# The second expert layer as one Strassen-type product over four experts, on one Trainium2 core

## The chip, the core and the metric

The kernel runs on one core of a Trainium2 chip. The core has engines that work side by side: TensorE (PE, with its weight loads listed apart as PEld), VectorE (DVE), ScalarE (ACT), GpSimd (POOL) and SyncE (SP, which here only issues DMAs). They wait for each other through semaphores. Matrix products are written to PSUM; DVE and ACT read them from there and write to SBUF. The metric is the time of one execution on the device in microseconds (us); smaller is better.

## What is computed

Attention over eight sorted blocks, whose output goes through a layer of four experts that are all used and mixed with normalised weights p. There are four batches of 768 tokens, 8 heads of 64, a model width of 512 and a hidden width of 1024.

```python
def _attn_ref(q, k, v, sort_net):
    ...
    for _ in range(5):
        P = P - np.max(P, axis=-1, keepdims=True)
        P = np.exp(P)
        P = P / (np.sum(P, axis=-1, keepdims=True) + 1e-09)
        P = P / (np.sum(P, axis=-2, keepdims=True) + 1e-09)
    k_sorted = np.einsum('bhij,bhjcd->bhicd', P, k_b).reshape(B, H, S, D)
    v_sorted = np.einsum('bhij,bhjcd->bhicd', P, v_b).reshape(B, H, S, D)
    ...
    scores = scale * np.matmul(q_b, k_sb.transpose(0, 1, 2, 4, 3))
    ...
    return np.matmul(attn, v_sb).reshape(B, H, S, D).astype(np.float32)

def _moe_ref(x, domain_probs, w1, w2):
    p = domain_probs / (domain_probs.sum(-1, keepdims=True) + 1e-09)
    ...
    for e in range(E):
        h = np.maximum(x @ w1[e], 0.0)
        out += p[:, e:e + 1] * (h @ w2[e])
    return out.astype(np.float32)
```

## The kernel before

All four experts' weights are brought to SBUF in f16 (`load_w1` and `load_w2`, lines 94 to 98) by DMAs that POOL issues. So are q, k and v of a batch (`load_natural`, line 79), in tiles with two buffers of a whole batch each, so that the next batch is loaded while one is worked on.

The attention of a batch is cut into small stages: `st_v`, `st_q`, `st_k` bring v, q and k into the layouts needed, `st_s` makes the scores and their exponentials, `st_a` the weighted sums, which `normalize` (line 334) divides on DVE, and `st_x` transposes the result into `xT`, the input of the experts. `attention_order` (line 464) lists the 24 stages of a batch. Batch 0 has stages of its own (`h_k` to `h_x`) that work on half a batch (`hf`).

`expert` (line 488) computes one expert for 768 tokens (`hf` is None, batches 1 to 3) or for 384 (batch 0). The first layer takes w1 as the stationary operand and 384 tokens as the moving one; after eight matmuls ACT writes relu of the two PSUM banks to `hT` as f16 (lines 504 and 520). The second layer takes 128 tokens of `hT` as the stationary operand and 512 columns of w2 as the moving one, sums eight matmuls in a PSUM bank, and DVE adds p times that to `oacc` (lines 535 and 539). After the last expert the rows go to DRAM from SP's queue.

`run` (line 555) threads the attention stages of the next batch into the experts of the present one: after each piece of expert work it calls `slot`, which issues as many stages as keep pace with the share of expert work done. The kernel is scheduled by hand: each engine executes its instructions in the order in which they are written. Lines 590 to 621 are the outer order: POOL builds the sort matrices (`build_PI`, lines 232 to 251) and loads what comes next, then batch 0's units run in two calls of `run`, then batches 1 to 3 in one call each. Batch 3's has no stages left to thread in.

PSUM has two pools of two buffers, each of two banks: `psM` for the experts and `psA` for attention.

Of the kernel before, what the change touches and what calls it, by code (L numbers as in the profile page):

```python
# [17 lines left out]
def kernel(  # L18
# [41 lines left out]
    moeo = ctx.enter_context(tc.tile_pool(name="moeo", bufs=9))  # L60
# [18 lines left out]
    def load_natural(b, nm, lo, n, p0=0, pn=P):  # L79
# [4 lines left out]
        nc.gpsimd.dma_start(  # L84
            t[ds(p0, pn), ds(lo, n), :, :].rearrange("p h r d -> p h (r d)"),
            src[b, ds(lo, n)].rearrange("h (p r) d -> p h (r d)", r=R)[ds(p0, pn)],
        )

# [11 lines left out]
    load_natural(0, "k", 0, 4)  # L100
    load_natural(0, "q", 0, 4, 0, P // 2)
# [4 lines left out]
    load_natural(0, "v", 0, 4)  # L106
    load_natural(0, "k", 4, 4)
    load_natural(0, "v", 4, 4)
    load_natural(0, "q", 4, 4, 0, P // 2)
    load_natural(0, "q", 0, H, P // 2, P // 2)  # L110
# [10 lines left out]
    )  # L121
    kTs, ETs, vos, vs0s = [], [], [], []
# [8 lines left out]
    for n in range(2):  # L131
        vs0 = att.tile([BLK, HB, 2, 2, VW], F16, name=f"vs0_{n}", tag="vs")
        nc.gpsimd.memset(vs0[:, :, :, :, ds(D, 2)], 1.0)
        vs0s.append(vs0)
# [3 lines left out]
    load_w2(1)  # L138
    nc.gpsimd.tensor_copy(
# [3 lines left out]
    for n in range(2):  # L143
# [26 lines left out]
    def q_half(b, pr, hf, copy):  # L170

        ps = psa([P, R, 64], F16, f"ps_q_{b}_{pr}_{hf}")
        for r in range(R):
            for hh in range(2):
                nc.tensor.transpose(
                    ps[ds(D * hh, D), r, :],
                    natural[(b, "q")][ds(64 * hf, 64), 2 * pr + hh, r, :],
                    ident[ds(64 * hf, 64), ds(64 * hf, 64)],
                )
        if (b, pr) not in qTs:  # L180
            qTs[(b, pr)] = att.tile([P, NB, R * CP], F16, name=f"qT_{b}_{pr}", tag="qT", bufs=4)
        copy(
            qTs[(b, pr)][:, ds(HB * hf, HB), :].rearrange("p i (r c) -> p i r c", r=R),
            ps.rearrange("p r (i c) -> p i r c", c=CP),
        )
# [36 lines left out]
    PI0 = [const.tile([P, H, HB, CP], F16, name=f"PI0_{a}") for a in range(2)]  # L222
# [11 lines left out]
    def build_PI(eng, n, which):  # L234
        r4 = Rs[:, ds(4 * n, 4), :]
        if which == "k":
            PIk[n] = att.tile([P, 4, NB, CP], F16, name=f"PIk_{n}", tag="PIk", bufs=4)
            eng.tensor_tensor(  # L238
                PIk[n][:],
                maskk.rearrange("p (o i c) -> p o i c", o=1, c=CP).broadcast_to([P, 4, NB, CP]),  # L240
                r4.rearrange("p g (i o) -> p g i o", o=1).broadcast_to([P, 4, NB, CP]),
                ALU.mult,
            )
        else:
            PIv[n] = att.tile([P, 4, CP, NB], F16, name=f"PIv_{n}", tag="PIv", bufs=4)
            eng.tensor_tensor(
                PIv[n][:],
                maskv.rearrange("p (o c i) -> p o c i", o=1, i=NB).broadcast_to([P, 4, CP, NB]),
                r4.rearrange("p g (o i) -> p g o i", o=1).broadcast_to([P, 4, CP, NB]),
                ALU.mult,  # L250
            )
# [8 lines left out]

    def st_v(b, pr):
        ps = psa([P, 2, 512], F32, f"ps_v_{b}_{pr}")
        for hh in range(2):
            h = 2 * pr + hh
            nc.tensor.matmul(  # L265
                ps[:, hh, 0:R * D],
                PIv[(b * H + h) // 4][:, h % 4, :, :].rearrange("p c i -> p (c i)"),
                natural[(b, "v")][:, h, :, :].rearrange("p r d -> p (r d)"),
                start=True, stop=True,
            )  # L270
        vo = vos[pr // 2]
        nc.vector.tensor_copy(  # L272
            vo[:, :, ds(2 * (pr % 2), 2), 0:D],
            ps[:, :, 0:R * D].rearrange("p h (r d) -> p r h d", r=R),
        )
        if pr % 2:
            qd = pr // 2
            nc.sync.dma_start(
                vs_dram[b, qd].rearrange("r c i x -> (c i) r x"),
                vo.rearrange("p r h w -> p r (h w)"),  # L280
            )
            vs = att.tile([BLK, NB, 4, VW], F16, name=f"vs_{b}_{qd}", tag="vs")
            nc.sync.dma_start(
                vs.rearrange("c i h w -> c (i h w)"),
                vs_dram[b, qd].rearrange("r c i x -> (r c) (i x)"),
            )
            vss[(b, qd)] = vs

    def st_q(b, pr):
        ps = psa([P, R, P], F16, f"ps_q_{b}_{pr}")  # L290
        for r in range(R):
            for hh in range(2):
                nc.tensor.transpose(  # L293
                    ps[ds(D * hh, D), r, :], natural[(b, "q")][:, 2 * pr + hh, r, :], ident[:]
                )
        qT = att.tile([P, NB, R, CP], F16, name=f"qT_{b}_{pr}", tag="qT", bufs=4)
        nc.vector.tensor_copy(qT[:], ps.rearrange("p r (i c) -> p i r c", c=CP))  # L297
        qTs[(b, pr)] = qT.rearrange("p i r c -> p i (r c)")

    def st_k(b, pr):  # L300
        ps = psa([P, R, P], F32, f"ps_k_{b}_{pr}")
        for r in range(R):
            for hh in range(2):
# [3 lines left out]
                    natural[(b, "k")][:, h, r, :],  # L307
# [4 lines left out]
        nc.vector.tensor_copy(  # L312
# [49 lines left out]
    def st_x(b, pr):  # L362
# [8 lines left out]
        nc.vector.tensor_copy(  # L371
# [7 lines left out]
    vT0, xsl0 = {}, {}  # L379

    def mix_half(nm, qd, hf, dst, copy):

        ps = psa([P, 2, R, 64], F32, f"ps_m{nm}_{qd}_{hf}")
        for sg in range(2):
            for r in range(R):
                for hh in range(2):
# [3 lines left out]
                        natural[(0, nm)][:, h, r, :],  # L390
# [11 lines left out]
    def h_v(qd, hf):  # L402
        vT = att.tile([P, S], F16, name=f"vT_{qd}_{hf}", tag="vT")
        vT0[(qd, hf)] = vT
        mix_half("v", qd, hf, vT, nc.scalar.copy)

    def h_w(qd, hf):
        ps = psa([BLK, 2 * HB, P], F16, f"ps_w_{qd}_{hf}")
        vT = vT0[(qd, hf)]
# [54 lines left out]
    def attention_order(b):  # L464
# [11 lines left out]
        return [lambda f=f, pr=pr: f(b, pr) for f, pr in o]  # L476


    def mix_weights():
# [4 lines left out]
        nc.vector.tensor_tensor(p_sb[:], p_sb[:], den[:].broadcast_to([P, B, R, E]), ALU.mult)  # L484

    oaccs = {}

    def expert(b, e, hf, slot):

        n = S if hf is None else HS  # L490
        hT = moe.tile([P, NFC, n], F16, name=f"hT_{b}_{e}_{hf}", tag="hT")
        if hf is None:
            xT = xTs[b].rearrange("p k r i c -> p k (r i c)")
            for fc in range(NFC):
                ps = psm([P, 2, 512], F32, f"ps_h_{b}_{e}_{fc}")
                for nh in range(2):
                    for kc in range(NKC):
                        nc.tensor.matmul(  # L498
                            ps[:, nh, 0:HS],
                            w1sb[e][:, kc, ds(fc * P, P)],  # L500
                            xT[:, kc, ds(nh * HS, HS)],
                            start=(kc == 0), stop=(kc == NKC - 1),
                        )
                nc.scalar.activation(  # L504
                    hT[:, fc, :].rearrange("p (a x) -> p a x", a=2), ps[:, :, 0:HS],
                    AF.Relu, bias=0.0, scale=1.0,
                )
                slot()
        else:
# [14 lines left out]
        for t in range(n // P):  # L524
            col = t if hf is None else (R // 2) * hf + t
# [17 lines left out]
            if e == E - 1:  # L543
                oacc = oaccs[(b, col)]
                if hf is None:
                    nc.sync.dma_start(
                        out[ds(b * S, S), :].rearrange("(p r) d -> p r d", r=R)[:, t, :], oacc[:]
                    )
                else:
                    o = out[ds(b * S + hf * HS, HS), :].rearrange("(p r s) d -> p r s d", r=R // 2, s=2)  # L550
                    for s2 in range(2):
                        nc.sync.dma_start(o[:, t, s2, :], oacc[ds(64 * s2, 64), :])
            slot()

    def run(units, fill, spare=4):

        slots = sum((NFC + R) if hf is None else (NFC // 2 + R // 2) for _, _, hf in units)
# [8 lines left out]
        for b, e, hf in units:  # L566
            expert(b, e, hf, slot)
        for f in fill:
            f()

# [37 lines left out]
    run([(0, 0, 0), (0, 1, 0)], second, 2)  # L608
    run(
        [(0, 0, 1), (0, 1, 1), (0, 2, 0), (0, 2, 1), (0, 3, 0), (0, 3, 1)],  # L610
        attention_order(1),
    )
    for b in range(1, B):
        if b + 1 < B:
            for nm in ("k", "v", "q"):
                load_natural(b + 1, nm, 0, H)
        if b + 2 < B:
            for n in range(2 * b + 4, 2 * b + 6):
                build_PI(nc.gpsimd, n, "v")
                build_PI(nc.gpsimd, n, "k")  # L620
        run([(b, e, None) for e in range(E)], attention_order(b + 1) if b + 1 < B else [])


# [28 lines left out]
```

## Time and profile before

| | |
|---|---|
| median of 3 runs | 416.14 us (413.9 to 416.29) |
| the profiled execution | 414.46 us |
| its span, first to last instruction | 412.6 us |
| mean granted TensorE clock | 0.982 |
| batch 0, with the attention of batch 1 | 0 to 137.1 us |
| batches 1 and 2, with attention of the next | 137.1 to 231.4, 231.4 to 325.8 us |
| batch 3, experts alone | 325.8 to 412.6 us |

The profile is one execution, recorded by the hardware. A group row reads: line, engine, operation, output<-input by the program's names, partitions x elements and type, count | busy time in us, mean ns of one | idle time of the engine before them, and what ended most of it. The chain that ended last is read from the last instruction back: at each step stands what released the instruction, or the one ahead of it on its engine; its rows give start, length, and what it was. Matmuls are pipelined: a mean of 379 ns for one of 512 columns contains time in which its neighbours run too, so the pace of a stream is read from the chain, as length over count.

### The profile page before, as it was taken

The numbers are of one execution on the slowest core, as the hardware profiler recorded it, in microseconds if no ns is written. First come the engines' busy times: TensorE is split into PE (matmuls) and PEld (weight loads), VectorE is DVE, ScalarE is ACT, GpSimd is POOL, SyncE is SP. The second block draws the span as 40 slices with busy tenths as digits, with TensorE's granted clock in tenths as the row PEclk, the third lists the DMA queues.
The fourth block names the chain that finished last, engine by engine and source line by source line (L and its number), as shares of the span: only waits on it lengthen the run. The fifth ranks groups of instructions, "written<-read, shape, count | busy, mean of one in ns | idle before, by whom it ended". The sixth has DMA issues, their size and how long they took to land.

```text
span 412.6 us, 7014 instructions
## 1 busy us (share of the span) xinstructions
PE 395.3 (96%) x3148; PEld 221.1 (54%) x3148; DVE 154.2 (37%) x259; ACT 135.6 (33%) x177; POOL 36.5 (9%) x63
## 2 busy tenths in 40 slices
PE   5679989999999999999999999999999999999996
PEld 5655545555555555546465554646555555555552
DVE  5374444354434334252434434343344212131313
ACT  2344233432343332606042232515233141414140
POOL 8386101010030000000000000000000000000000
PEclk9959999999999999999999999999999999999999
DMA  9999999930079412000001222000000300000003
GB/s 118 206 209 205 208 210 208 227 84 2 0 101 207 100 56 79 2 2 0 2 2 51 103 79 80 2 0 2 0 2 27 127 2 1 0 2 0 2 15 138
DMA packets 29054, 29.49 MB, mean 71 GB/s; under 512 B 2336, under 2 KB 23328, under 8 KB 29024
## 3 DMA queue, kind: packets, MB, share of 16 engines
q0 software_dynamic: 18816, 17.83, 26.7%
q1 hardware_dynamic: 10208, 11.22, 8.9%
q8 instruction: 24, 0.39, 0.4%
q14 instruction: 6, 0.05, 0.0%
HBM read 38.14 MB, written 8.72 MB: 114 GB/s over the span
## 4 chain that ended last, share of the span: by engine, by line
PE 91%; DVE 3%; DMA 3%; ACT 1%; POOL 1%; issue 1%; ACTq 0%; POOLq 0%
PE ps_o L528 41%; PE ps_h L498 31%; PE ps_h L514 10%; DMA nat_q<-in_q_dram 3%; DVE xsl L339 2%; PE ps_s L322 1%; PE ps_q L293 1%; PE ps_k L305 1%; PE ps_a L354 1%; PE ps_x L368 1%; PE ps_v L265 1%; PE ps_x L456 1%; ACT ET L430 1%; PE ps_s L423 0%; DVE kT L394 0%
## 5 line engine op out<-in xcount | busy, mean ns | idle before, releaser
L498 PE MATMUL ps_h<-xT,w 128*128 128x384 f16 x768 | 131.5, 326 | 0.0
L504 ACT ACTIVATE hT_None<-ps_h 128x768 f16<-128x768 f32 x96 | 77.9, 811 | 156.6 <-PE ps_h L498 156.6
L528 PE MATMUL ps_o<-w,hT_None 128*128 128x512 f16 x576 | 128.3, 379 | 0.0
L498 PEld LDWEIGHTS <-w 128*128 128x128 f16 x768 | 73.0, 98 | 48.3
L539 DVE SCALAR_TENSOR_TENSOR oacc<-ps_o,p_sb,oacc 128x512 f32<-128x512 f32 x72 | 54.1, 751 | 119.6 <-PE ps_o L528 119.6
L528 PEld LDWEIGHTS <-hT_None 128*128 128x128 f16 x576 | 55.5, 98 | 64.6
L514 PE MATMUL ps_h<-xT,w 128*128 128x384 f16 x256 | 47.2, 332 | 0.2 <-ACT xT L459 0.2
L520 ACT ACTIVATE hT<-ps_h 128x768 f16<-128x768 f32 x32 | 26.0, 811 | 62.4 <-PE ps_h L514 62.4
L528 PE MATMUL ps_o<-w,hT 128*128 128x512 f16 x192 | 44.5, 380 | 0.0
L514 PEld LDWEIGHTS <-w 128*128 128x128 f16 x256 | 24.1, 99 | 16.2 <-issue 1.5
L535 DVE TENSOR_SCALAR oacc<-ps_o,p_sb 128x512 f32<-128x512 f32 x24 | 18.0, 751 | 35.9 <-PE ps_o L528 35.9
L528 PEld LDWEIGHTS <-hT 128*128 128x128 f16 x192 | 17.6, 98 | 19.7 <-ACT hT L520 0.3
L329 ACT ACTIVATE ET<-ps_s 96x768 f16<-96x768 f32 x24 | 18.0, 802 | 21.3 <-PE ps_s L322 21.3
L339 DVE TENSOR_TENSOR xsl<-ps_a,rz 96x512 f16<-96x512 f32 x32 | 22.0, 687 | 1.1
L312 DVE CAST kT<-ps_k 128x768 f16<-128x768 f32 x12 | 11.4, 954 | 13.4 <-PE ps_k L305 13.4
L371 DVE COPY xT<-ps_x 128x768 f16<-128x768 f16 x12 | 6.7, 555 | 25.0 <-PE ps_x L368 25.0
L272 DVE CAST vo<-ps_v 128x768 f16<-128x768 f32 x12 | 11.4, 954 | 7.5 <-PE ps_v L265 7.5
L338 DVE RECIPROCAL rz<-ps_a 96x8 f32<-96x8 f32 x32 | 6.3, 197 | 20.5 <-PE ps_a L354 17.1
L297 DVE COPY qT<-ps_q 128x768 f16<-128x768 f16 x12 | 6.6, 552 | 12.1 <-PE ps_q L293 12.1
L168 PE MATMUL ps_w<-ident 128*128 128x128 f16 x76 | 7.8, 295 | 3.4 <-POOL ident masks.py:199 3.4
L238 POOL TENSOR_TENSOR PIk<-maskk,Rs 128x512 f16<-128x512 f16 x6 | 6.3, 1053 | 45.9 <-PE ps_k L305 45.9
L168 PEld LDWEIGHTS <-ident 128*128 128x128 f16 x76 | 7.3, 139 | 3.5 <-POOL ident masks.py:199 3.4
(73 smaller groups left out, 174.6 us busy)
## 6 DMA issues: line engine op xcount, KB each, us to landing
w<-in_moe_w_dram POOLq DMA_DIRECT2D x8, 1024.0 KB, 23.3
out_dram<-oacc SPq DMA_DIRECT2D x18, 256.0 KB, 2.0
vs_dram<-vo SPq DMA_DIRECT2D x6, 396.0 KB, 3.6
vs<-vs_dram SPq DMA_DIRECT2D x6, 396.0 KB, 3.5
nat_k<-in_k_dram POOLq DMA_DIRECT2D x3, 768.0 KB, 19.0
nat_v<-in_v_dram POOLq DMA_DIRECT2D x3, 768.0 KB, 22.0
nat_q<-in_q_dram POOLq DMA_DIRECT2D x3, 768.0 KB, 25.0
out_dram<-oacc SPq DMA_DIRECT2D x12, 128.0 KB, 3.8
```

Of the source, the lines that this page charges most:

```text
L168: nc.tensor.matmul(ps[:, m % 4, :], ident[:], ident[:], start=True, stop=True)
L272: nc.vector.tensor_copy(vo[:, :, ds(2 * (pr % 2), 2), 0:D], ps[:, :, 0:R * D].rearrange("p h (r d) -> p r h d", r=R),)
L312: nc.vector.tensor_copy(kT[:, 0:S].rearrange("p (i r c) -> p i r c", i=NB, r=R), ps.rearrange("p r (i c) -> p i r c", c=CP),)
L329: nc.scalar.activation(ETs[2 * (pr % 2) + hh][:, 0:S].rearrange("c (a x) -> c a x", a=2), pss[hh][0:BLK, :, 0:HS], AF.Exp, bias=0.0, scale ...
L339: nc.vector.tensor_tensor(xsl[:, :, hh, :].rearrange("c (a i) d -> c a i d", a=2), av[:, :, :, 0:D], rz[:].broadcast_to([BLK, 2, HB, D]), ...
L498: nc.tensor.matmul(ps[:, nh, 0:HS], w1sb[e][:, kc, ds(fc * P, P)], xT[:, kc, ds(nh * HS, HS)], start=(kc == 0), stop=(kc == NKC - 1),)
L504: nc.scalar.activation(hT[:, fc, :].rearrange("p (a x) -> p a x", a=2), ps[:, :, 0:HS], AF.Relu, bias=0.0, scale=1.0,)
L514: nc.tensor.matmul(ps[:, a, 0:HS], w1sb[e][:, kc, ds((2 * f2 + a) * P, P)], xT0[hf][:, :, kc, :], start=(kc == 0), stop=(kc == NKC - 1),)
L520: nc.scalar.activation(hT[:, ds(2 * f2, 2), :], ps[:, :, 0:HS], AF.Relu, bias=0.0, scale=1.0,)
L528: nc.tensor.matmul(ps[:], hT[:, fc, ds(t * P, P)], w2sb[e][:, fc, :], start=(fc == 0), stop=(fc == NFC - 1),)
L535: nc.vector.tensor_scalar(out=oaccs[(b, col)][:], in0=ps[:], scalar1=pcol, scalar2=None, op0=ALU.mult)
L539: nc.vector.scalar_tensor_tensor(out=oaccs[(b, col)][:], in0=ps[:], scalar=pcol, op0=ALU.mult, in1=oaccs[(b, col)][:], op1=ALU.add,)
```

## The change

In batches 1 to 3 the second layer is computed for 256 tokens at a time (a chunk, three to a batch) as one product whose inner dimension runs over the hidden units of all four experts. For this h is scaled by p: DVE takes max(h, 0) times p from PSUM and writes it to `Hb` as f16, in place of ACT's relu. p, which must now vary along the free dimension, is transposed once (`spread_weights`), written to DRAM and read back for each chunk, broadcast to all partitions (`load_p`).

The product of a 2 x 2 block matrix (256 tokens by the two halves of each expert's hidden units) with another (these halves by two halves of 256 output columns) is made in seven block multiplications instead of eight, by Winograd's form of Strassen's scheme. Its sums of weights are made once per expert by POOL (`weight_sums`), one of them in place. Its four sums of h per expert and chunk are made by DVE in f16 (`h_sums`), those of an expert between the evacuations of the next. Each of the seven products sums 16 matmuls of 256 columns in PSUM; ACT, DVE and POOL combine them into two output tiles of 128 rows. The first layer of these batches runs over 256 tokens too.

To make room in SBUF, q, k and v are held in tiles of four heads with one batch's worth of buffers in all, reloaded by `load_natural` after the stage that last reads them; batch 0's temporary tiles and hidden layers lie in the new `Sb` and `Hb`; several tiles have fewer buffers. Batch 1's loads come behind the building of its sort matrices, and the loads of w1 and w2 of experts 2 and 3 stay behind these. The evacuations of the attention of batches 2 and 3 move from DVE to ACT (`evac`). Batch 0's expert units are computed as before.

```diff
-    moeo = ctx.enter_context(tc.tile_pool(name="moeo", bufs=9))
+    moeo = ctx.enter_context(tc.tile_pool(name="moeo", bufs=6))
...
-        if (b, nm) not in natural:
-            natural[(b, nm)] = nat.tile([P, H, R, D], F16, name=f"nat_{nm}_{b}", tag=f"nat_{nm}")
-        t = natural[(b, nm)]
+        if (b, nm, qd) not in natural:
+            natural[(b, nm, qd)] = nat.tile([P, 4, R, D], F16, name=f"nat_{nm}_{b}_{qd}", tag=f"nat_{nm}")
+        t = natural[(b, nm, qd)]
...
-    load_natural(0, "q", 0, H, P // 2, P // 2)
+    for qd in range(2):
+        load_natural(0, "q", qd, P // 2, P // 2)
...
+    KH = NFC // 2
+    Hb = const.tile([P, E, NFC, 2 * P], F16, name="Hb")
+    Sb = const.tile([P, 4, E, KH * P], F16, name="Sb")
...
-            PIk[n] = att.tile([P, 4, NB, CP], F16, name=f"PIk_{n}", tag="PIk", bufs=4)
+            PIk[n] = att.tile([P, 4, NB, CP], F16, name=f"PIk_{n}", tag="PIk")
...
+    def evac(b):
+        return nc.vector.tensor_copy if b == 1 else nc.scalar.copy
...
-        vo = vos[pr // 2]
-        nc.vector.tensor_copy(
+        vo = vos[0]
+        evac(b)(
...
+        def stage(f, pr):
+            f(b, pr)
+            nm = {st_q: "q", st_k: "k", st_v: "v"}.get(f)
+            if nm and pr % 2 and b + 1 < B:
+                load_natural(b + 1, nm, pr // 2)
...
+    def spread_weights():
+        ps = psa([NR, P], F32, "ps_p")
+        nc.tensor.transpose(ps[:], pn[:], identf[:])
+        nc.vector.tensor_copy(pT[:], ps[:])
+        nc.sync.dma_start(p_dram.rearrange("b e (r p) -> (b e r) p", p=P), pT[:])
+        pbs[(1, 0)] = load_p(1, 0)
...
+    def weight_sums(e):
+        t = const.tile([P, 3, KH, DH], F16, name=f"T_{e}")
+        w = w2sb[e]
+        b11, b12 = w[:, 0:KH, 0:DH], w[:, 0:KH, DH:Dm]
+        b21, b22 = w[:, KH:NFC, 0:DH], w[:, KH:NFC, DH:Dm]
+        t2, t3, n4 = t[:, 0], t[:, 1], t[:, 2]
+        tt = nc.gpsimd.tensor_tensor
+        tt(t3, b22, b12, ALU.subtract)
+        tt(b12, b12, b11, ALU.subtract)
+        tt(t2, b22, b12, ALU.subtract)
+        tt(n4, b21, t2, ALU.subtract)
...
+    def load_p(b, c):
+        pb = moe.tile([P, E, 2 * P], F32, name=f"pb_{b}_{c}", tag="pb", bufs=1)
+        nc.sync.dma_start(
+            pb[:],
+            p_dram[b - 1, :, ds(2 * c * P, 2 * P)].rearrange("(o e) x -> o e x", o=1).broadcast_to([P, E, 2 * P]),
+        )
+        return pb
+
+    def h_sums(e, which):
+        blk = lambda kh, tok: Hb[:, e, ds(kh * KH, KH), ds(tok * P, P)]
+        sm = [Sb[:, n, e].rearrange("p (f x) -> p f x", f=KH) for n in range(4)]
+        tt = nc.vector.tensor_tensor
+        if which == 1:
+            tt(sm[0], blk(0, 1), blk(1, 1), ALU.add)
+        elif which == 2:
+            tt(sm[1], sm[0], blk(0, 0), ALU.subtract)
+        elif which == 3:
+            tt(sm[2], blk(0, 0), blk(0, 1), ALU.subtract)
+        else:
+            tt(sm[3], blk(1, 0), sm[1], ALU.subtract)
...
+    def chunk(b, c, slot):
+        xT = xTs[b].rearrange("p k r i c -> p k (r i c)")
+        pb = pbs.pop((b, c))
+        for e in range(E):
+            for g in range(2):
+                ps = psm([P, 4, 2 * P], F32, f"ps_h_{b}_{c}_{e}_{g}")
+                for f in range(4):
+                    for kc in range(NKC):
+                        nc.tensor.matmul(
+                            ps[:, f, :],
+                            w1sb[e][:, kc, ds((4 * g + f) * P, P)],
+                            xT[:, kc, ds(2 * c * P, 2 * P)],
+                            start=(kc == 0), stop=(kc == NKC - 1),
+                        )
+                nc.vector.scalar_tensor_tensor(
+                    out=Hb[:, e, ds(4 * g, 4), :], in0=ps[:], scalar=0.0,
+                    op0=ALU.max, in1=pb[:, ds(e, 1), :].broadcast_to([P, 4, 2 * P]), op1=ALU.mult,
+                )
+                if e:
+                    h_sums(e - 1, 1 + 2 * g)
+                    h_sums(e - 1, 2 + 2 * g)
+                slot()
+        for w in range(1, 5):
+            h_sums(E - 1, w)
+        if (b, c) != (B - 1, R // 2 - 1):
+            nxt = (b, c + 1) if c + 1 < R // 2 else (b + 1, 0)
+            pbs[nxt] = load_p(*nxt)
...
+        def product(n, lhs, rhs):
+            ps = psm([P, DH], F32, f"ps_{n}_{b}_{c}")
+            for e in range(E):
+                for f in range(KH):
+                    nc.tensor.matmul(
+                        ps[:], lhs(e, f), Ts[e][rhs][:, f, :],
+                        start=(e == 0 and f == 0), stop=(e == E - 1 and f == KH - 1),
+                    )
+            slot()
+            return ps[:]
...
+        nc.scalar.copy(p1[:], product("p1", blk(0, 0), "b11"))
+        nc.scalar.copy(ob1, product("p4", blk(1, 1), "n4"))
+        tt(oa1, product("p2", blk(1, 0), "b21"), p1[:], ALU.add)
+        nc.scalar.copy(p5[:], product("p5", sm(0), "t1"))
+        tt(u2[:], product("p6", sm(1), "t2"), p1[:], ALU.add)
+        nc.gpsimd.tensor_tensor(oa2, u2[:], p5[:], ALU.add)
+        tt(u3[:], product("p7", sm(2), "t3"), u2[:], ALU.add)
+        nc.gpsimd.tensor_tensor(ob2, u3[:], p5[:], ALU.add)
+        tt(ob1, ob1, u3[:], ALU.add)
+        nc.sync.dma_start(o[:, 2 * c + 1, :], ob[:])
+        tt(oa2, product("p3", sm(3), "b22"), oa2, ALU.add)
+        nc.sync.dma_start(o[:, 2 * c, :], oa[:])
...
-    for nm in ("k", "v", "q"):
-        load_natural(1, nm, 0, H)
-    for n in range(2, 6):
+    for n in range(2, 4):
         build_PI(nc.gpsimd, n, "v")
         build_PI(nc.gpsimd, n, "k")
+    for qd in range(2):
+        for nm in ("k", "v", "q"):
+            load_natural(1, nm, qd)
...
+    first = attention_order(1)
     run(
-        [(0, 0, 1), (0, 1, 1), (0, 2, 0), (0, 2, 1), (0, 3, 0), (0, 3, 1)],
-        attention_order(1),
+        halves([(0, 0, 1), (0, 1, 1)]) + plain(lambda: weight_sums(0), lambda: weight_sums(1))
+        + halves([(0, 2, 0), (0, 2, 1), (0, 3, 0)]) + plain(lambda: weight_sums(2)) + halves([(0, 3, 1)]),
+        6 * SLOTS, first[:10] + [spread_weights] + first[10:],
     )
+    builds(2)
+    weight_sums(3)
     for b in range(1, B):
-        if b + 1 < B:
-            for nm in ("k", "v", "q"):
-                load_natural(b + 1, nm, 0, H)
...
-        run([(b, e, None) for e in range(E)], attention_order(b + 1) if b + 1 < B else [])
+        fill = attention_order(b + 1) if b + 1 < B else []
+        if b > 1 and fill:
+            builds(b + 1)
+        run(
+            [lambda slot, b=b, c=c: chunk(b, c, slot) for c in range(R // 2)],
+            (R // 2) * (2 * E + 7), fill,
+        )
```

More of the change, by code (lines that the diff above doesn't have):

```diff
@@ L553, in expert @@
             slot()
-    def run(units, fill, spare=4):
-        slots = sum((NFC + R) if hf is None else (NFC // 2 + R // 2) for _, _, hf in units)
+            return ps[:]
+        oa = moeo.tile([P, Dm], F32, name=f"oa_{b}_{c}", tag="oacc")
+        ob = moeo.tile([P, Dm], F32, name=f"ob_{b}_{c}", tag="oacc")
+        p1, p5, u2, u3 = [moe.tile([P, DH], F32, name=f"{n}_{b}_{c}", tag=n, bufs=1) for n in ("p1", "p5", "u2", "u3")]
+        tt = nc.vector.tensor_tensor
+        o = out[ds(b * S, S), :].rearrange("(p r) d -> p r d", r=R)
```

138 lines of the change are left out of this document (74 added, 64 removed).

## Prediction

> **What bounds the kernel now.** I read the page's totals first, then the busy time by stretches, then the chain of work that ended last, and only then the groups by form.
>
> ```profile
> span 412.6 us, 7014 instructions
> ...
> PE 395.3 (96%) x3148; PEld 221.1 (54%) x3148; DVE 154.2 (37%) x259; ACT 135.6 (33%) x177; POOL 36.5 (9%) x63
> ```
>
> The busy time by stretches (after the length come PE, PEld, DVE, ACT, POOL) shows the runs of batch 2 and batch 3; that of batch 1 looks like batch 2's:
>
> ```profile
> 231.40:325.80 94.40, 94.40 (x714) 51.30 (x712) 36.26 (x56) 31.38 (x40) 0.00 (x0) 1.00 0.11 35
> 325.80:412.60 86.80, 83.06 (x449) 43.64 (x446) 18.77 (x25) 25.95 (x32) 0.00 (x0) 0.99 0.07 25
> ```
>
> PE is busy all the time there, at a granted clock of 1.00, while DVE and ACT are idle for more than half of it. So in batches 1 to 3 a microsecond taken from PE is a microsecond of the span, and time added to DVE or ACT costs nothing until it makes PE wait. The chain of waits gives clean prices for the two products, from batch 3, where nothing else is on PE:
>
> ```profile
> 325.82 10.40 PE ps_h L498 x64
> 336.22 10.36 PE ps_o L528 x48
> ...
> 398.50 10.37 PE ps_o L528 x48
> 408.90 0.75 DVE oacc L539
> ```
>
> A matmul with 384 columns takes 10.40/64 = 0.1625 us, one with 512 takes 10.36/48 = 0.2158 us. The difference, 0.0533 us for 128 columns, gives 0.1092 us for 256 columns, the size that the change uses throughout. The evacuation starts 0.03 us after the last matmul (398.50 + 10.37 = 408.87).
>
> **Part 1: PE's work.** From the groups by form:
>
> ```profile
> L498 PE MATMUL ps_h<-xT,w 128*128 128x384 f16 x768 | 131.5, 326 | 0.0
> L528 PE MATMUL ps_o<-w,hT_None 128*128 128x512 f16 x576 | 128.3, 379 | 0.0
> ...
> L539 DVE SCALAR_TENSOR_TENSOR oacc<-ps_o,p_sb,oacc 128x512 f32<-128x512 f32 x72 | 54.1, 751 | 119.6 <-PE ps_o L528 119.6
> ...
> L354 PE MATMUL ps_a<-vs,ET 96*128 96x65 f16 x192 | 7.8, 193 | 0.0
> L354 PEld LDWEIGHTS <-ET 96*128 96x128 f16 x192 | 7.4, 97 | 1.9
> ```
>
> Second layer: 576 x 0.2158 = 124.3 us go. Per chunk of 256 tokens there are seven products of 4 experts x 4 row blocks = 112 matmuls; nine chunks make 1008 x 0.1092 = 110.1 us. Gain 14.2 us (one eighth is 15.5; 1.3 goes to the shorter matmuls). First layer: 768 x 0.1625 = 124.8 us become 9 x 128 = 1152 x 0.1092 = 125.8 us, 1.0 us lost. Could the weight loads, now one per 256 columns, be the limit? The 16 ps_a matmuls of one stage load 128 columns of weights each and take 0.49 us together:
>
> ```profile
> 264.11 0.49 PE ps_a L354 x16
> ```
>
> That is 0.031 us for a load and a matmul of 65 columns, so a load hides easily under 0.109 us. I take no cost (upper end: 0.01 us more for each of 2160 matmuls, 22 us, were a load to show; no row speaks for it).
>
> **Part 2: DVE's new work.** Evacuating h leaves ACT and becomes one DVE instruction of 128x1024 from PSUM per group of 16 matmuls, eight per chunk. DVE also makes 16 f16 sums of 128x512 per chunk, all operands in SBUF. The price rows, all DVE:
>
> ```profile
> L312 DVE CAST kT<-ps_k 128x768 f16<-128x768 f32 x12 | 11.4, 954 | 13.4 <-PE ps_k L305 13.4
> L371 DVE COPY xT<-ps_x 128x768 f16<-128x768 f16 x12 | 6.7, 555 | 25.0 <-PE ps_x L368 25.0
> ...
> L182 DVE COPY qT<-ps_q 128x384 f16<-128x384 f16 x4 | 1.4, 352 | 3.1 <-PE ps_q L175 3.1
> ...
> L227 DVE TENSOR_TENSOR PI<-maskk,ps_R 128x512 f16<-128x512 f16 x1 | 0.7, 689 | 1.5 <-PE ps_R L216 1.5
> ...
> L580 DVE CAST Rs<-ps_R 128x256 f16<-128x256 f32 x1 | 0.4, 410 | 0.0
> ```
>
> From PSUM in f32 an element costs (954 - 410)/512 = 1.06 ns. The evacuation is 751 + 512 x 1.06 = 1.29 us from the three-operand row (L539), 1.23 from the CAST row; I take 1.29. For a sum, the f16 copies give (555 - 352)/384 = 0.53 ns an element, so 0.42 us for 512; the TENSOR_TENSOR that reads PSUM (L227) took 0.69. No row has this form. I take 0.42, because the copies are nearest in type (all f16), and keep 0.69 as the other end. [...]
>
> Neighbours on DVE overlap a little, as the timeline of one normalisation shows:
>
> ```profile
> 170.03 0.20 DVE L338 RECIPROCAL rz<-ps_a 96x8 f32<-96x8 f32 x1 [1.99 <-PE ps_a L354]
> 170.26 0.69 DVE L339 TENSOR_TENSOR xsl<-ps_a,rz 96x512 f16<-96x512 f32 x1
> 170.87 0.19 DVE L338 RECIPROCAL rz<-ps_a 96x8 f32<-96x8 f32 x1
> 171.10 0.69 DVE L339 TENSOR_TENSOR xsl<-ps_a,rz 96x512 f16<-96x512 f32 x1
> ```
>
> An independent neighbour starts 0.08 us before the end (170.87 against 170.95), a dependent one about 0.04 after it. So an evacuation occupies 1.21, a sum 0.34; one normalisation stage 1.7.
>
> Now one chunk of batch 3, time from its first matmul. A group is 16 x 0.1092 = 1.75 us of PE, psM has two buffers, and from the third group on DVE has 1.21 plus two sums: 0.80 in the even groups, where the second sum needs the first, 0.68 in the odd ones. So DVE's period is 2.01 or 1.89 against PE's 1.75. Evacuations of groups 2 to 7 start at 5.28, 7.29, 9.18, 11.19, 13.08, 15.09. Group 6 waits for the end of evacuation 4 (10.47) and starts at 10.52 in place of 10.48, group 7 at 12.53, product p1 at 14.42 (end of evacuation 6, 14.37). p4 needs evacuation 7 (16.38) and starts at 16.43. The last expert's four sums end at 18.46, before p2 does (19.92), so nothing more waits. The chunk ends at 26.91 against 26.21 of pure PE work: 0.70 us lost, 2.1 in batch 3. In batches 1 and 2 attention stages add PE time to this phase (0.45 us each) and the normalisation adds DVE time: chunk 0 has five stages and no normalisation, no loss; chunk 1 has 2.3 us of PE against 1.7 of DVE, no loss; chunk 2 has two normalisations, 3.4 against 2.3, and loses some 1.3. Stalls in all: 2.1 + 2 x 1.3 = 4.7 us.
>
> That p1 may start before the last evacuation supposes that a wait concerns the part of a tile that is read. It does: PE's timeline has ps_o reading hT before ACT's last write of it begins.
>
> ```profile
> 336.06 10.52 PE L528 MATMUL ps_o<-w,hT_None 128*128 128x512 f16 x48
> ```
> ```profile
> 336.26 0.81 ACT L504 ACTIVATE hT_None<-ps_h 128x768 f16<-128x768 f32 x1 [0.49 <-PE ps_h L498]
> ```
>
> **Part 3: loads and POOL.** Batch 1's q, k, v now wait for batch 0's buffers, and the loads of w1 and w2 for experts 2 and 3 are queued behind the last of them.
>
> ```profile
> 33.74 0.82 POOL L95 DMA_DIRECT2D w<-in_moe_w_dram  x1
> ...
> 50.01 0.88 POOL L84 DMA_DIRECT2D nat_q<-in_q_dram  x1 [4.07 <-PE ps_q L175]
> ```
> ```profile
> w<-in_moe_w_dram POOLq DMA_DIRECT2D x8, 1024.0 KB, 23.3
> ...
> vs<-vs_dram SPq DMA_DIRECT2D x6, 396.0 KB, 3.5
> ```
> ```profile
> 87.20 1.30 PE ps_h L514 x8
> ```
>
> The last buffer frees at 50.0 (batch 2's q load waits for it today), so the four weight loads go from 33.7 to 51 to 54 and land by about 54 + 23 = 77. Expert 2 begins at 87.2. Covered; without that cover PE would wait for the whole lateness. The load of p, 512 KB per chunk on SP's queue, starts once the last evacuation has read the old copy (16.4) and is needed at 28.7: 12 us for what the 396 KB row puts at about 5.
>
> POOL makes four sums of 128x1024 per expert:
>
> ```profile
> L246 POOL TENSOR_TENSOR PIv<-maskv,Rs 128x512 f16<-128x512 f16 x6 | 6.3, 1054 | 15.2 <-PE ps_v L265 15.2
> ```
>
> (Group rows of POOL are rough.) Twice the elements, at most 2.1 us each, 8.4 for an expert. The last expert's start when batch 0 ends, at 137, and end by 146; p4 of chunk 0 needs them at about 155. Covered by the first product. The two POOL adds per chunk lie under p7 and p3 (1.75 each). Smaller edits: one vo buffer (a wait of about 1 us on DVE in batch 0, while ACT serves the first product), one more DMA issue at the head, the transposition of p. I take 0.5 us, between 0 and 2. The last DVE add is half as long: -0.3.
>
> **Sum.** 412.6 - 14.2 + 1.0 + 4.7 + 0.5 - 0.3 = 404.3 us of span. The profiled run took 414.46 us, 1.86 more than its span: 406.2. It lies 1.7 us under the median of the runs (416.14); halfway between 406.2 and 407.9 I say 407.0.
>
> **Rivals.** (a) The f16 sums run like L227, at 0.69 us: DVE becomes the bound of each first product. The periods are 2.55 and 2.43, p4 starts at 19.1 and a chunk loses 3.4 us: 10.2 in batch 3, and with attention (1.5, 2.9 and 4.5 in the three chunks) 8.9 in batches 1 and 2. Stalls 28 in place of 4.7: 430 us, slower. Between the two ends the loss is some 86 us per microsecond of a sum; the gain is gone at about 0.52 us. For it: the only DVE tensor_tensor on f16 in the trace took 0.69. Against: it read PSUM, and the all-f16 copies ran at twice that rate.
>
> (b) The mechanism holds, but DVE is less dense than I took it (no overlap of neighbours, more wait when normalisations fall between evacuations). Without the 0.08 us overlap a period grows by 0.2, p4 starts 1.1 later in batch 3, stalls grow by about 5: 412 us. With sums at 0.48 it is 411 to 416, within 1%.
>
> (c) DVE's period stays under PE's 1.75, which it does with 1.21 for the evacuation and sums of 0.32 at most: no stall, 412.6 - 13.2 - 0.3 + 1.9 = 401 us. No row speaks for so short a sum, and none excludes it.
>
> (d) POOL and DVE hinder each other. While POOL multiplied, DVE instructions with all operands in SBUF were long:
>
> ```profile
> 28.58 3.23 DVE L482 TENSOR_SCALAR den<-den 128x24 f32<-128x24 f32 x1
> ```
> ```profile
> 28.71 1.05 POOL L238 TENSOR_TENSOR PIk<-maskk,Rs 128x512 f16<-128x512 f16 x1
> ```
>
> Such are the new sums. POOL's weight sums of expert 3 overlap the first DVE sums of batch 1 by at most one instruction (about 2 us), and the two adds per chunk meet only DVE's output adds; if all eighteen (about 0.6 us) held up the chain it would be 11 us: 417 us, no change. [...]
>
> **Chances.** The forecast (403 to 411) 0.60, (c) 0.08, (b) 0.16, (a) 0.12, (d) 0.04. About 1%, 4 us, is what a measurement of this kernel can tell from no change. Faster by over 1% (under 412): the forecast, (c), none of the rest: 0.68. Within 1%: (b) and (d) but for a part: 0.17. Slower: (a) and the far end of (b): 0.15. Range 401 to 416, which leaves out (a), (d) and little else.
>
> **What would show it.** Right: 256-column matmuls at 0.109 us; 72 evacuations of 1.29 and 144 sums of 0.42; batch 3 in three chunks of about 26.9 us; a short PE wait before p4 of each chunk; no PE wait on w or nat. Wrong: sums near 0.69, PE waiting on DVE in every group, waits on POOL's weight sums in the first chunk, or on p.

## The result, and the profile after

The changed kernel takes 404.12 us (median of 4 runs, 403.17 to 405.32) against 416.13 before; the ratio, taken over all the runs and not from the two medians, is 0.9725, with a 95% interval of 0.9682 to 0.9768. In two further sets of runs it took 403.93 (ratio 0.9736, 0.9721 to 0.9751) and 404.6 (0.9772, 0.9753 to 0.9791). One execution of the first further set (after_again, the one that was profiled) took 1364.68 us, its matmuls some 3.8 times as long (PE was busy for 480.4 us with the 1152 of 256 columns in the first layer, which at 0.1092 each make 125.8), and one of the kernel before 467.82; the ratios are without these two. The change is faster by 2.3 to 2.8%; 407.0 was forecast, within 401 to 416. The profiled execution took 403.17 us with a span of 401.4, 11.2 less than before.

The page's totals after the change (busy time, share of the span, instructions):

```profile
span 401.4 us, 8931 instructions
...
PE 380.6 (95%) x3965; PEld 298.0 (74%) x3965; DVE 233.4 (58%) x418; ACT 93.9 (23%) x140; POOL 89.8 (22%) x107
```

PE lost 14.7 us of busy time and is still the bound; DVE gained 79 us, ACT lost 42, POOL gained 53 (34 of it the sums of weights). PEld's 77 us more are the weight loads of shorter matmuls; they overlap (in batch 3's 79.90 us below PE is busy for 79.83 and PEld for 70.28), and no pace shows them: in sums_once a matmul of 256 columns takes 0.1092 us, as forecast without a cost for them. The chain of waits in batch 3 (start, length, what):

```profile
344.34 14.12 PE ps_h L629 x128
358.45 1.80 PE ps_p L656 x16
360.26 0.02 issue
360.27 10.64 PE ps_p L656 x96
...
397.50 0.03 issue
397.53 0.02 DVEq L679
397.55 0.04 issue
397.60 0.42 DVE oa L679
```

One chunk lasts from 344.34 to 370.92, 26.58 us. The busy time by stretches of batches 1, 2 and 3 (length, then PE, PEld, DVE, ACT, POOL):

```profile
136.18:226.90 90.72, 90.16 (x986) 77.85 (x985) 59.76 (x103) 21.87 (x33) 14.99 (x16) 1.00 0.38 80
226.90:317.60 90.70, 90.14 (x986) 77.93 (x984) 60.01 (x104) 21.86 (x33) 8.29 (x10) 1.00 0.17 54
317.60:397.50 79.90, 79.83 (x722) 70.28 (x719) 53.23 (x88) 3.35 (x9) 4.35 (x6) 1.00 0.11 34
```

Against 94.40 for a batch with attention before, 3.7 us each are gained, and 3.3 in batch 3 (three chunks of 26.58, against 83.06). And the groups that were priced in advance (mean ns behind the busy time):

```profile
L635 DVE SCALAR_TENSOR_TENSOR Hb<-ps_h,pb 128x1024 f16<-128x1024 f32 x72 | 87.8, 1220 | 24.4 <-PE ps_h L629 24.3
...
L612 DVE TENSOR_TENSOR Sb<-Sb,Hb 128x512 f16<-128x512 f16 x36 | 15.3, 425 | 1.2
L616 DVE TENSOR_TENSOR Sb<-Hb,Sb 128x512 f16<-128x512 f16 x36 | 15.0, 417 | 0.0
L614 DVE TENSOR_TENSOR Sb<-Hb 128x512 f16<-128x512 f16 x36 | 14.9, 415 | 0.0
L610 DVE TENSOR_TENSOR Sb<-Hb 128x512 f16<-128x512 f16 x36 | 14.9, 414 | 0.0
...
L589 POOL TENSOR_TENSOR T<-w 128x1024 f16<-128x1024 f16 x4 | 8.5, 2130 | 0.0
```

A sum costs 0.414 to 0.425 us (0.42 forecast), an evacuation 1.22 (1.29), a POOL sum 2.12 to 2.13 (2.1).

### The profile page after: what moved, and what is told of

Read it like the earlier page. It is cut to its first block, busy times and chain, and to the rows that moved or that the text cites. A ratio compares the mean times of both kernels' runs of the same rounds, so it can differ in the third digit from the quotient of the medians.

```text
span 401.4 us, 8931 instructions
## 1 busy us (share of the span) xinstructions
PE 380.6 (95%) x3965; PEld 298.0 (74%) x3965; DVE 233.4 (58%) x418; ACT 93.9 (23%) x140; POOL 89.8 (22%) x107
## 3 DMA queue, kind: packets, MB, share of 16 engines
q1 hardware_dynamic: 15044, 15.97, 13.2%
## 4 chain that ended last, share of the span: by engine, by line
PE 80%; DVE 10%; DMA 5%; POOL 1%; issue 1%; ACT 1%; DVEq 0%; POOLq 0%; SPq 0%; ACTq 0%
PE ps_h L629 27%; PE ps_p L656 26%; PE ps_o L554 9%; PE ps_h L540 9%; DVE Hb L635 3%; DMA vs_dram<-vo 3%; DMA nat_q<-in_q_dram 3%; DVE xsl L361 2%; PE ps_k L327 1%; PE ps_q L315 1%; PE ps_s L344 1%; PE ps_x L390 1%; PE ps_a L376 1%; PE ps_v L287 1%; DVE Sb L612 1%
## 5 line engine op out<-in xcount | busy, mean ns | idle before, releaser
L629 PE MATMUL ps_h<-xT,w 128*128 128x256 f16 x1152 | 132.0, 273 | 1.0 <-DVE Hb L635 1.0
L629 PEld LDWEIGHTS <-w 128*128 128x128 f16 x1152 | 111.2, 98 | 16.0 <-issue 1.4
L635 DVE SCALAR_TENSOR_TENSOR Hb<-ps_h,pb 128x1024 f16<-128x1024 f32 x72 | 87.8, 1220 | 24.4 <-PE ps_h L629 24.3
L656 PEld LDWEIGHTS <-Sb 128*128 128x128 f16 x576 | 55.6, 98 | 7.0
L540 PE MATMUL ps_h<-xT,w 128*128 128x384 f16 x256 | 47.0, 332 | 0.2 <-ACT xT L480 0.2
L656 PEld LDWEIGHTS <-Hb 128*128 128x128 f16 x432 | 41.6, 98 | 5.9 <-issue 0.6
L554 PE MATMUL ps_o<-w,Hb 128*128 128x512 f16 x192 | 44.4, 379 | 0.0
L540 PEld LDWEIGHTS <-w 128*128 128x128 f16 x256 | 24.1, 99 | 16.1 <-issue 1.5
L656 PE MATMUL ps_p<-w,Sb 128*128 128x256 f16 x288 | 34.4, 273 | 0.0
L656 PE MATMUL ps_p<-w,Hb 128*128 128x256 f16 x288 | 34.4, 273 | 0.0
L554 PEld LDWEIGHTS <-Hb 128*128 128x128 f16 x192 | 17.6, 98 | 19.8 <-ACT Hb L546 0.6
L565 DVE SCALAR_TENSOR_TENSOR oacc<-ps_o,p_sb,oacc 128x512 f32<-128x512 f32 x18 | 13.5, 751 | 26.8 <-PE ps_o L554 26.8
```

The lines of the kernel that those rows point to most:

```text
L540: nc.tensor.matmul(ps[:, a, 0:HS], w1sb[e][:, kc, ds((2 * f2 + a) * P, P)], xT0[hf][:, :, kc, :], start=(kc == 0), stop=(kc == NKC - 1),)
L554: nc.tensor.matmul(ps[:], hT[:, fc, ds(t * P, P)], w2sb[e][:, fc, :], start=(fc == 0), stop=(fc == NFC - 1),)
L565: nc.vector.scalar_tensor_tensor(out=oaccs[(b, col)][:], in0=ps[:], scalar=pcol, op0=ALU.mult, in1=oaccs[(b, col)][:], op1=ALU.add,)
L629: nc.tensor.matmul(ps[:, f, :], w1sb[e][:, kc, ds((4 * g + f) * P, P)], xT[:, kc, ds(2 * c * P, 2 * P)], start=(kc == 0), stop=(kc == NKC ...
L635: nc.vector.scalar_tensor_tensor(out=Hb[:, e, ds(4 * g, 4), :], in0=ps[:], scalar=0.0, op0=ALU.max, in1=pb[:, ds(e, 1), :].broadcast_to([P ...
L656: nc.tensor.matmul(ps[:], lhs(e, f), Ts[e][rhs][:, f, :], start=(e == 0 and f == 0), stop=(e == E - 1 and f == KH - 1),)
```

## The experiments

Theory A is that of the prediction: seven block products in place of eight take 14.2 us from PE, and DVE, only a little slower than PE in the first layer's product ("the first product" below), gives some of it back. Its rivals are named where they are tested.

Spans are a poor measure of a few tenths here. The head of the kernel, until batch 1 begins, took between 135.6 us (sums_once) and 138.0 us (after_third) in kernels whose heads are the same, and 135.0 (late_pool_w) and 135.2 (evac_pointer) in two whose heads differ a little. So I compare the stretch from the first matmul of batch 1 to the last of batch 3, from the rows of each trace. There is one trace of each kernel, and two of the changed one, from different sets of runs, which agree:

| kernel | stretch, us | against the changed kernel |
|---|---|---|
| before (136.91 to 408.87) | 272.0 | +10.6 |
| changed (136.18 to 397.50) | 261.3 | |
| changed, in after_third (138.03 to 399.35) | 261.3 | 0.0 |
| eight_products | 272.9 | +11.6 |
| sums_once | 258.6 | -2.7 |
| evac_pointer | 263.2 | +1.8 |
| sums_half_more | 272.8 | +11.5 |
| sums_twice | 307.8 | +46.5 |
| sums_late | 260.3 | -1.0 |
| sums_pool | 259.7 | -1.6 |
| w_first | 261.3 | 0.0 |
| late_pool_w | 259.7 | -1.6 |

**The change itself, again** (after_again, after_third), to stand beside the others:

> The changed kernel unchanged, to stand beside the others on the same chip. Span 401 to 404 us, batch 3's chunks 26.6 us each, f16 sums 0.42 us.

> The changed kernel unchanged, beside the next three on one chip: span 401 to 404 us.

403.93 and 404.6 us, as given above. In the trace of after_third the chunks of batch 3 take 26.57 us and the f16 sums 0.42.

**Is it the saved product?** eight_products: the same chunks, but the ordinary second layer.

```diff
-        nc.scalar.copy(p1[:], product("p1", blk(0, 0), "b11"))
...
-        tt(oa2, product("p3", sm(3), "b22"), oa2, ALU.add)
+        for tok in range(2):
+            ps = psm([P, Dm], F32, f"ps_y_{b}_{c}_{tok}")
+            for e in range(E):
+                for f in range(NFC):
+                    nc.tensor.matmul(
+                        ps[:], Hb[:, e, f, ds(tok * P, P)], w2sb[e][:, f, :],
+                        start=(e == 0 and f == 0), stop=(e == E - 1 and f == NFC - 1),
+                    )
...
+            nc.scalar.copy(ot[:], ps[:])
```

> The chunks of batches 1 to 3 keep the scaled h and the sum over all experts in PSUM, but the second layer is made in the ordinary way: 64 matmuls of 512 columns per chunk, no sums of weights, no sums of h. Theory A (the gain is the eighth of the block products that is saved): 64 x 0.2158 = 13.8 us per chunk in place of 12.2, nine times 1.6 is 14.2 more, less some 2.5 of stalls that go with the sums: span about 413, as slow as before the change. Rival B (the gain comes from scaling h and summing the experts in PSUM, which frees DVE of 512-column accumulations): span 399 to 403, batch 3 no longer than now.

Measured: 416.1 us, span 414.3; the kernel before took 414.83 on that chip. Its chain in batch 3:

```profile
382.56 13.97 PE ps_h L629 x128
396.53 13.83 PE ps_y L652 x64
```

The second layer of a chunk takes 13.83 us in place of 12.2, PE has no waits, and the stretch is 11.6 longer (11.7 forecast). Scaling h and summing the experts in PSUM gains nothing by itself; rival B is out, and the gain is the saved eighth of the block products. The stretch is 0.9 us above that of the kernel before, which is about what the first layer's shorter matmuls were forecast to cost (1.0).

**What do the sums cost?** sums_once makes them in the first chunk only.

```diff
-                if e:
+                if e and (b, c) == (1, 0):
...
-            h_sums(E - 1, w)
+            if (b, c) == (1, 0):
+                h_sums(E - 1, w)
```

> The sums of h are made in the first chunk only and left out in the other eight, whose products use the first chunk's. Theory A: no wait is left in these, batch 3 takes 78.7 us in place of 79.7, span 398.5 to 399.5; this is all that the sums cost. If PE's first product is slowed by something else (256 columns, p, the evacuations themselves), the span stays above 400.5.

```profile
341.83 13.97 PE ps_h L629 x128
355.81 12.23 PE ps_p L657 x112
```

399.91 us. Chunks of batch 3 take 26.20 us, which is 128 and 112 matmuls at 0.1092 each: without the sums nothing is left but the matmuls. The stretch is 2.7 us shorter, so all of DVE's sums together cost 2.7 us (0.4 for each chunk of batch 3, which is 1.1 for that batch and leaves some 0.8 for each of batches 1 and 2). Against eight_products the stretch is 14.3 us shorter: that is what the saved products are worth, 14.2 by the forecast.

**Why was the evacuation shorter than forecast?** evac_pointer:

```diff
+    zero = const.tile([P, 1], F32, name="zero")
+    nc.vector.memset(zero[:], 0.0)
...
-                    out=Hb[:, e, ds(4 * g, 4), :], in0=ps[:], scalar=0.0,
+                    out=Hb[:, e, ds(4 * g, 4), :], in0=ps[:], scalar=zero[:, 0:1],
```

> The evacuation of h takes its zero from a column in SBUF, one value per partition, in place of a constant in the instruction; the numbers are the same. Theory C (the 0.07 us by which the forecast of 1.29 was too long is the reading of such a column, which the row it came from had): the evacuation takes 1.28 to 1.29, batch 3's chunks 26.9 in place of 26.6, span about 403.5. Otherwise it stays at 1.22 and the span at 401.4.

```profile
L637 DVE SCALAR_TENSOR_TENSOR Hb<-ps_h,zero,pb 128x1024 f16<-128x1024 f32 x72 | 92.0, 1280 | 22.0 <-PE ps_h L631 20.9
```

1.280 in place of 1.220 us, chunks of batch 3 at 26.95 us, stretch +1.8; span 402.3 with a head some 0.9 us shorter. Reading a scalar column costs 0.06 us per instruction here, and that alone raises the waits from 2.7 to 4.5 us, the forecast being 4.7.

**How steep is the price of a sum?** sums_twice makes each sum twice; sums_half_more puts one of half the size into an unread tile before each.

```diff
-                    h_sums(e - 1, 1 + 2 * g)
-                    h_sums(e - 1, 2 + 2 * g)
+                    for w in (1 + 2 * g, 2 + 2 * g):
+                        h_sums(e - 1, w)
+                        h_sums(e - 1, w)
...
         for w in range(1, 5):
+            h_sums(E - 1, w)
             h_sums(E - 1, w)
```
```diff
+        tt(extra[:], Hb[:, e, 0:2, 0:P], Hb[:, e, 2:4, 0:P], ALU.add)
         if which == 1:
...
+    extra = const.tile([P, KH // 2, P], F16, name="extra")
```

> Each sum of h is made twice, so a sum costs about 0.76 us in place of 0.42. Theory A with DVE just above PE's pace: DVE's period in the first product goes from 1.9 to 2.5, the fourth product of a chunk starts 3.2 us later in batch 3, some 3 in the others: span 424 to 430, and PE waits for the evacuation of h in every group. If the sums are hidden whatever they cost: under 405.

> Each sum of h is preceded by a sum of half the size into a tile that nobody reads: some 0.21 us more of DVE per sum, without the wait that two writes of one tile had. Forecast's rival (a) put the price at 86 us per microsecond of a sum: 18 us more, span 419, past the point where the gain is gone (0.52 us a sum; here 0.55 to 0.63). If the doubled sums were dear for another reason than DVE's period: under 410.

sums_twice took 450.63 us, far above what was expected. DVE's timeline has the reason; it shows a group of twins as one row of two:

```profile
362.33 1.22 DVE L635 SCALAR_TENSOR_TENSOR Hb<-ps_h,pb 128x1024 f16<-128x1024 f32 x1
363.46 0.87 DVE L610 TENSOR_TENSOR Sb<-Hb 128x512 f16<-128x512 f16 x2
364.37 0.88 DVE L612 TENSOR_TENSOR Sb<-Sb,Hb 128x512 f16<-128x512 f16 x2
365.17 1.22 DVE L635 SCALAR_TENSOR_TENSOR Hb<-ps_h,pb 128x1024 f16<-128x1024 f32 x1
```

Two twins, which write one tile, take 0.87 to 0.88 us together, where independent neighbours start 0.33 us apart (L614 and L616 in the changed kernel): the second runs behind the first and not beside its end, so a twin adds some 0.45 us and not 0.34, and DVE's period is 2.84 us (362.33 to 365.17) against PE's 1.75. And the normalisations of attention stand in DVE's queue behind all that, so PE waits for them as well, which I had left out (the waits of PE, in total, times, longest):

```profile
PE ps_h L629 <- DVE Hb L635: 15.9, 24, 0.9
PE ps_s L344 <- DVE xsl L361: 7.5, 7, 2.5
PE ps_p L658 <- DVE Hb L635: 6.7, 11, 0.8
```

sums_half_more took 415.11 us with a span of 413.3, where 419 was expected:

```profile
359.40 0.28 DVE L609 TENSOR_TENSOR extra<-Hb 128x256 f16<-128x256 f16 x1
359.60 0.42 DVE L611 TENSOR_TENSOR Sb<-Hb 128x512 f16<-128x512 f16 x1
```

The extra half sum takes 0.28 us by itself, 0.20 beside its neighbours, and costs 11.5 us. So the price is no straight line: the first 0.20 us cost 11.5, the next 0.25 cost 35. The chunks show where it bends. In batch 3, without attention, each grows by 1.64 us for 0.20 more per sum and by 4.58 for 0.45, roughly in proportion; batches 1 and 2 lose some 3.3 us each for 0.20 and 16.4 for 0.45. At some 0.2 us more per sum (0.62 against 0.42) the gain of the change is gone.

**Can the rest of the waits be had?** sums_late moves the third expert's sums behind the last evacuation; sums_pool gives the third and fourth sum to POOL; w_first issues the weight loads ahead of batch 1's q, k, v; late_pool_w does all three, and takes the last eight sums in another order (both third sums first).

```diff
-                if e:
+                if e in (1, 2):
                     h_sums(e - 1, 1 + 2 * g)
                     h_sums(e - 1, 2 + 2 * g)
                 slot()
-        for w in range(1, 5):
-            h_sums(E - 1, w)
+        for s in (E - 2, E - 1):
+            for w in range(1, 5):
+                h_sums(s, w)
```
```diff
         elif which == 3:
+            tt = nc.gpsimd.tensor_tensor
             tt(sm[2], blk(0, 0), blk(0, 1), ALU.subtract)
         else:
+            tt = nc.gpsimd.tensor_tensor
             tt(sm[3], blk(1, 0), sm[1], ALU.subtract)
```
```diff
+    for e in range(2, E):
+        load_w1(e)
+        load_w2(e)
     for qd in range(2):
         for nm in ("k", "v", "q"):
             load_natural(1, nm, qd)
-    for e in range(2, E):
-        load_w1(e)
-        load_w2(e)
```

> The sums of the third expert move behind the last evacuation of the chunk; nothing else changes. Theory A (what is left of the stalls is the wait of the fourth product for the last evacuation): that evacuation starts 0.8 us earlier, batch 3 loses 1 us, batches 1 and 2 some 0.7 each: span 399 to 400. If the sums are then late for the fifth product instead, no change: 401.4.

> The third and fourth sum of each expert move from DVE to POOL. DVE then needs 3.1 us per expert against PE's 3.5. If DVE and POOL run side by side: no wait is left, span 399 to 400. Rival D (a DVE instruction with two inputs in SBUF and one of POOL exclude each other): DVE's sums become longer by up to the 1.05 us of one POOL sum, and the span stays at 401 or goes up to 408.

> The loads of w1 and w2 of experts 2 and 3 are issued ahead of batch 1's q, k and v. Theory: in the changed kernel vo's way to DRAM took 11 us in batch 0 because these loads ran then, DVE waited 2.6 us for it and PE 0.5. That wait goes: 0.5 us less in batch 0, if q, k, v of batch 1 are not late instead (then PE waits on nat at about 62 us).

> Three edits together: the third expert's sums after the last evacuation, the third and fourth sum on POOL, the weight loads first. The floor, without sums, is 2.7 us under the changed kernel; this should come within 1 us of it, and 0.5 us for the loads: span 398.5 to 399.5, time 0.6 to 0.8% under the changed kernel. If POOL and DVE hold each other up, no better than the third expert's sums alone.

sums_late: 402.25 us (ratio to before 0.9699, 0.9675 to 0.9723, beside 0.9736 for the changed kernel on that chip), stretch -1.0 where 2.4 were expected: the fourth block product no longer waits, but the last group of the first product still does. sums_pool: 402.68, stretch -1.6; the chunks of batch 3 take 26.20 us as in sums_once, though some of DVE's sums became longer:

```profile
L615 POOL TENSOR_TENSOR Sb<-Hb 128x512 f16<-128x512 f16 x36 | 42.5, 1179 | 22.2 <-DVE Hb L637 14.9 <-DVE rz L360 7.3
...
L612 DVE TENSOR_TENSOR Sb<-Sb,Hb 128x512 f16<-128x512 f16 x36 | 19.5, 541 | 1.2
L610 DVE TENSOR_TENSOR Sb<-Hb 128x512 f16<-128x512 f16 x36 | 17.4, 483 | 0.2
```

DVE's sums rose from 0.414 and 0.425 to 0.483 and 0.541 us on average. These means mix two cases: 64 of the 72 sums take 0.42 us as before, and eight take 0.91 to 1.40, each while POOL makes a sum. POOL's sums take 1.15 us, and 1.33 in five such meetings. So what rival D supposes is seen on these eight sums, but most of the time the two do not meet. w_first: 403.67; vo's slowest way to DRAM is 6.8 us (7.9 in late_pool_w) where it is 10.5 to 11.6 in the kernels with the old order, and q, k, v are not late. PE's wait behind vo's evacuation (0.5 us in the changed kernel) is gone, but it is also absent from sums_once and sums_late, which have the old order, and 1.0 in after_third; beside a head that varies by over 2 us the total shows nothing, and what the edit is worth stays open. late_pool_w: 401.89 us, ratio 0.9723 (0.97 to 0.9746), beside 0.9772 (0.9753 to 0.9791) for the changed kernel on the same chip: 0.7% under the changed kernel. Its stretch is that of sums_pool alone, so of its three edits only the sums on POOL show there, and its profiled span of 398.6, within the 398.5 to 399.5 expected, owes 1.2 us to a short head. Its batch 3 is at the floor:

```profile
342.32 13.97 PE ps_h L631 x128
356.29 12.23 PE ps_p L659 x112
```

The 1.1 us that it lacks to sums_once lie in batches 1 and 2, where normalisations still fall between the evacuations and PE waits 0.5 us for an evacuation in each.

## The prediction, step by step

- **PE's work: right.** A 256-column matmul was read as 0.1092 us; the floor chunk of sums_once is 240 of them in 26.20 us, 0.1092 each. Of the 13.2 us forecast net, sums_once shows all: its stretch is 13.3 under that of before. The weight loads do not show.
- **The f16 sums: right**, at 0.42 us, the end that the all-f16 copies gave. The whole instruction takes 0.42 us against the 0.69 of L227, and an element 0.53 ns (0.280 us for 256 in sums_half_more, 0.415 for 512) against the 1.06 that the prediction reads for f32 from PSUM. Independent neighbours start 0.33 us apart, as L614 and L616 do (360.14 to 360.47). Why L227 took longer no run shows: it reads PSUM, but so do the f16 copies.
- **The evacuation and the stalls: the mechanism right, the size off.** The term was "Stalls in all: 4.7 us"; it measured 2.7. The step that failed was the price of the evacuation, 1.29 us taken from the three-operand row and not 1.23 from the CAST row. The three-operand row reads a scalar column; evac_pointer shows that its 0.06 us make 1.8 of the 2.0 us of error, and with it the chunks of batch 3 are 26.95 us long, 26.91 by the forecast. So the waits were placed rightly. In the changed kernel the chunks are 26.58 us long, 0.38 above the floor. About half of this is the wait before p4, which starts 1.92 us after p1 for 1.75 us of matmuls and just after evacuation 7 (359.01 + 1.22 = 360.23); the other half lies in the last group before p1 and at p1 itself, which starts when evacuation 6 ends (357.08 + 1.22 = 358.30):

```profile
358.35 1.91 PE L656 MATMUL ps_p<-w,Hb 128*128 128x256 f16 x16
360.27 1.91 PE L656 MATMUL ps_p<-T,Hb 128*128 128x256 f16 x16
```
```profile
357.08 1.22 DVE L635 SCALAR_TENSOR_TENSOR Hb<-ps_h,pb 128x1024 f16<-128x1024 f32 x1
...
359.01 1.22 DVE L635 SCALAR_TENSOR_TENSOR Hb<-ps_h,pb 128x1024 f16<-128x1024 f32 x1
...
360.14 0.41 DVE L614 TENSOR_TENSOR Sb<-Hb 128x512 f16<-128x512 f16 x1
360.47 0.41 DVE L616 TENSOR_TENSOR Sb<-Hb,Sb 128x512 f16<-128x512 f16 x1
```

- **Batch 0: 0.5 us were added, 0.7 us were gained**, but batch 1 began between 135.6 and 138.0 us in kernels with the same head, so the sign means nothing. The forecast wait for the single vo buffer was there, longer than forecast: DVE waited 2.6 us, since vo took 11.1 us to DRAM beside the delayed weight loads, and PE 0.5. (The profile of this run puts DVE's wait down to a matmul that came last; in after_third, with 3.1 us, it names vo's DMA. That the weight loads are the cause is what w_first shows, with its 6.8 us.)

```profile
PE ps_s L344 <- DVE vo L294: 0.5, 1, 0.5
```
```profile
DMA to landing us min/median/max: 3.0/4.0/11.1
```

- **The tail: -0.3 forecast, +0.2 measured** (3.73 us from the last matmul to the end before, 3.90 after). Its cause stays open.
- **Loads of w and p, POOL's sums: covered, as forecast.** PE waits for none of them.
- **The sum:** 404.3 us of span forecast, 401.4 measured: 2.0 from the stalls and 1.2 from batch 0 are too much, 0.5 from the tail too little; the rest is rounding and PE's work. The 1.2 from batch 0 cannot be told from the spread of the heads, so that part of the forecast is neither borne out nor refuted.
- **Rival (a)**, sums at 0.69 us: not the case. Its slope of 86 us per microsecond was too steep at first (11.5 for 0.20, 57 per microsecond) and too flat later (46.5 for 0.45, 103), because the waits of attention join in. **Rival (b)**, DVE less dense: not the case; a sum that needs nothing of its neighbour starts some 0.08 us before its end, as taken (360.47 against 360.55, L616 after L614), and the stalls were smaller than forecast. **Rival (c)**, no stall: 401 is as far from 404.1 as the 407.0 of the forecast; it took sums_once to be rid of all the stalls. **Rival (d)**: DVE's adds that meet POOL's take 0.99 us and not 0.43, as the last section shows, but they lie under p3 and cost nothing: in sums_once they take 0.93 us on average, and its chunks of batch 3 are at the floor. Its evidence was read too widely: beside POOL the addition to `den` took 3.23 us and the multiplication by it 0.71 (0.18 and 0.26 in the changed kernel, where POOL is idle then), but the reciprocal between them, also wholly in SBUF, took 0.30 in both. And the addition to `den` reads one tile, each of the new sums two.

## What to carry to other kernels

When PE is the bound, count columns times the measured pace: a scheme that saves an eighth of the block products gains that eighth less what its shorter matmuls cost (14.3 us of 15.5 here, of which the waits for its sums took 2.7 back), if its sums fit beside PE. Whether they fit is a matter of the period of the engine that makes them, group by group, in its own order, with all that stands in that queue (2.84 us for DVE against 1.75 for PE in sums_twice, which was slower than the kernel before); near equality a few hundredths of a microsecond per instruction were worth microseconds in the sum (0.06 us on each of 72 evacuations made 1.8 us in evac_pointer). And put into the queue first what PE waits for (evacuations), and sums that are needed later behind it (1.0 us in sums_late).

## What the hardware showed that I had not expected

A scalar operand read from a column in SBUF made a DVE instruction 0.06 us longer than a constant (1.280 against 1.220 for 128x1024). And DVE and POOL hindered each other, as in two adds that each read two tiles in SBUF. The changed kernel holds the comparison in itself, in the add L677 of each chunk (0.43 us alone, 0.99 to 1.00 beside POOL's add of 0.72). In the first chunk POOL has a DMA to issue ahead of its own add, and starts the add only after DVE's has ended; in the other eight the two start together, as here in the last chunk:

```profile
164.89 0.43 DVE L677 TENSOR_TENSOR ob<-ob,u 128x256 f32<-128x256 f32 x1
...
165.90 0.73 POOL L676 TENSOR_TENSOR ob<-u,p 128x256 f32<-128x256 f32 x1
```
```profile
396.34 0.72 POOL L676 TENSOR_TENSOR ob<-u,p 128x256 f32<-128x256 f32 x1 [1.02 <-DVE u L675]
396.35 0.99 DVE L677 TENSOR_TENSOR ob<-ob,u 128x256 f32<-128x256 f32 x1
```

The same instruction takes 0.43 us without POOL and 0.99 beside it, and ends 0.28 us after POOL's add (397.34 against 397.06). An add of this size with one input in PSUM takes 0.42 (L679). The addition to `den` that took 3.23 us during POOL's multiplications in the kernel before takes 0.18 in the changed kernel, with POOL idle:

```profile
28.01 0.18 DVE L523 TENSOR_SCALAR den<-den 128x24 f32<-128x24 f32 x1
```

DVE's add is 0.56 us longer beside a POOL add of 0.72, so some part of the two overlaps, and which part no row shows. The eight longer sums of sums_pool (0.91 to 1.40 us in place of 0.42) fall in the same way while POOL makes a sum.
